# Attention block and PReLU layer on one core: the second product as seven products of halves, all steps placed anew

## The chip, the cores and the metric

One core of one Trainium2 chip. The metric is the device time of one execution in microseconds (us). Engines are TensorE (PE; its weight loads PEld), VectorE (DVE), ScalarE (ACT), GpSimd (POOL) and SyncE (SP, which only starts DMAs). TensorE writes its results to PSUM, here eight banks of 128 partitions by 512 f32 values; GpSimd works only on SBUF.

## The reference

```python
# x: 8 batches, 8 heads, 512 tokens, 64;  state: 8, 8, 32, 64
scores = scale * x @ state.T ;   a  = softmax(scores)  ; xread = a @ state
scores2 = scale * state @ x.T ;  a2 = softmax(scores2) ; sread = a2 @ x
X = concat([xread, sread], over tokens)      # 8 x (512 + 32) rows of 8*64 = 512
h = X @ w_in                                  # 512 -> 2048
g = max(h, 0) + alpha * min(h, 0)
out = g @ w_out                               # 2048 -> 512, f32
```

## The kernel before

The work goes batch by batch, and the 32 state rows of all eight batches (the "reads", 256 rows) make a ninth batch, number 8. Matmul operands are f16, PSUM is f32.

**One order written by hand.** ORDER (L17 to 99) is a list of steps; the loop at L666 runs it from the top, and each engine gets its instructions in that order and executes them in that order. A step is a name with arguments: `F.4.10.2` is the first product of batch 4, tile 10 of the 16 blocks of 128 of the 2048 columns, into bank k2. The steps that matter here:

- `lx` (L159) loads x of a batch from GpSimd's queue, casting to f16, into one of four xg buffers; `wi`, `wo` (L197, L203) load quarters of w_in and w_out the same way. `xd` (L276) transposes x by a DMA of SP's queue; `xt`/`xo` do it on TensorE for batches 0 and 1.
- `sc` (L296) makes the scores on TensorE. Over the states: `sb` (transpose, L334), `smax` (maximum, L367), `ssh` (shift, L372, on GpSimd for batches 1 to 7), `sexp` (L381), `ssum` (L385, L386), `snorm` (L389, GpSimd), `wb` (transpose back, L397). Over the tokens: `tm` (maximum L409, and a 128x2 scaling by -scale, L412, on VectorE), `te` (L420), `tsum` (L430), `tn` (scaling of e by 1/sum, L434, GpSimd), `tt` (DMA transpose, L438), `rd` and `rdo` (reads, L453, L464).
- `m`/`mo` (L480; L504 whole or L506 half) make state @ w_in per batch and quarter f of the 2048 columns, in f16: xread @ w_in is then a @ m.
- `F` (L517; for the reads L526): h of one tile, 128 x 512 (reads 128 x 256), into a bank. `N` (L572): ScalarE writes neg = relu(-h). `G` (L580): VectorE makes g = neg * (1 - alpha) + h, f16. `f`, `n`, `g` are the same in halves for the first tiles of batch 0.
- `S` (L595): second product. For a quarter q of a batch's rows, 128 rows by 512 output columns in one bank, summed over the 16 tiles of g: 16 matmuls of 512 columns, two per step. `O` (L611): a copy to SBUF by ScalarE or VectorE and an output DMA by SP. `R`/`RO` (L636, L646) are the same for the reads, `V`/`VO` (L618, L628) the last 128 columns of the last quarter.
- `Z` (L224): matmuls of zeros at the start.

PSUM: single banks k0 to k5, and a pair "two". A step that opens a bank waits until what read it last is done.

Of the kernel before, what the change touches and what calls it, by code (L numbers as in the profile page):

```python
# [17 lines left out]
stc wi.0 Z.0.9 stt.0 sbd.0.a lst sto.a cx.0.1.v sbd.1.a lx.1 cx.0.0.v Z.1.5 xt.0.0.1.0 oma  # L18
xt.0.0.0.1 xo.0.0.1.v wi.1 cx.1.0.a xo.0.0.0.v cx.1.1.v wo.0 Z.2.6 xt.0.1.0.0 tsc.0.0.1 xo.0.1.0.v
tsc.0.1 xt.0.1.1.2 wi.2 smax.0.0 sc.0.0 tsc.1.0.0 xo.0.1.1.a wo.1 ssh.v.0.0 Z.3.2 tsc.1.1 sc.0.1  # L20
wi.3 smax.0.1 sexp.0.0 Z.2.5 m.0.0.1.2 tm.0 wo.2 mo.0.0.a.1 mo.0.0.a.0 ssh.v.0.1 te.0.1 Z.3.11
str.1.1 lx.2 ssum.0.0 str.0.0 sexp.0.1 sro.1.a ssum.0.1 snorm.p.0.0 te.0.0 snorm.p.0.1 Z.2.13 at.0.1
sro.0.a xt.1.1.0.2 tsum.0 ao.0.v xt.1.1.1.3 tn.0.1 xt.1.0.0.4 xo.1.1.1.v at.1.1 xo.1.1.0.a f.0.0.0.5
xo.1.0.0.v m.1.0 ao.1.v n.0.0.0 m.2.0.4.2 xt.1.0.1.3 mo.1.0.v wo.3 mo.2.0.a.1 f.0.0.1.1 xo.1.0.1.a
f.0.1.1.0 tn.0.0 g.0.0.0.1 n.0.0.1 m.1.1 g.0.0.0.0 n.0.1.1 g.0.0.1.1 m.0.1.5.3 mo.1.1.a g.0.1.1.0
lx.3 tt.0 g.0.0.1.0 mo.0.1.a.1 g.0.1.1.1 sc.1 f.0.1.0.1 mo.0.1.a.0 sb.1 S.0.3.0.0 mo.2.0.a.0 F.0.4.3
n.0.1.0 F.0.5.2 tm.1 N.0.4 S.0.2.0.4 N.0.5 S.0.3.1 S.0.1.0.5 G.0.5 te.1.1 S.0.1.1 g.0.1.0.1 te.1.0
F.0.7.2 g.0.1.0.0 G.0.4 N.0.7 m.0.2 S.0.2.1 G.0.7 F.0.6.3 mo.0.2.v S.0.2.2 N.0.6 S.0.1.2 S.0.3.2
G.0.6 F.0.9.2 F.0.10.1 smax.1 N.0.9 F.0.8.3 N.0.10 S.0.3.3 N.0.8 G.0.9 m.0.3 ssh.p.1 S.0.2.3
mo.0.3.a G.0.10 F.0.11.2 G.0.8 S.0.1.3 N.0.11 F.0.14.1 tsum.1 sexp.1 F.0.12.3 tn.1.0 G.0.11 S.0.2.4  # L30
N.0.14 S.0.3.4 ssum.1 S.0.1.4 N.0.12 tn.1.1 S.0.1.5 S.0.2.5 G.0.14 F.0.13.2 m.1.2 snorm.p.1 G.0.12
xd.2 N.0.13 S.0.0.0.1 mo.1.2.a S.0.0.1 G.0.13 S.0.0.2 F.0.15.2 wb.1 S.0.0.3 N.0.15 S.0.0.4 S.0.1.6
G.0.15 F.1.4.3 S.0.0.5 N.1.4 S.0.1.7 F.1.0.2 G.1.4 O.0.1.a S.0.0.6 N.1.0 F.1.2.3 S.0.2.6 G.1.0 N.1.2
F.1.3.5 F.1.5.2 G.1.2 N.1.3 tt.1 S.0.0.7 N.1.5 F.1.1.3 G.1.3 S.0.2.7 xd.3 N.1.1 G.1.5 F.1.10.5 m.1.3
O.0.0.v N.1.10 rd.0.2 O.0.2.v mo.1.3.a F.1.6.1 lx.4 G.1.10 S.0.3.5 rdo.0.a N.1.6 sc.2 G.1.1
m.2.2.5.2 F.1.9.4 mo.2.2.a.0 tm.2 F.1.8.3 mo.2.2.a.1 S.0.3.6 N.1.9 S.1.0.0.2 G.1.6 N.1.8 S.0.3.7
te.2.0 G.1.9 S.1.0.1 F.1.11.1 te.2.1 G.1.8 F.1.7.4 N.1.11 S.1.0.2 tsum.2 sb.2 tn.2.1 N.1.7 F.1.13.3
rd.1.5 O.0.3.a G.1.7 N.1.13 xd.4 m.3.2 S.1.1.0.0 rdo.1.a lx.5 G.1.11 mo.3.2.a S.1.0.3 smax.2
F.1.12.5 tn.2.0 S.1.1.1 N.1.12 m.2.1 G.1.13 m.2.3.1.4 S.1.0.4 mo.2.1.a G.1.12 ssh.p.2 F.1.15.3 tt.2
mo.2.3.a.0 S.1.0.5 mo.2.3.v.1 N.1.15 F.1.14.5 S.1.1.2 G.1.15 N.1.14 S.1.1.3 sexp.2 S.1.1.4 G.1.14  # L40
S.1.0.6 sc.3 ssum.2 m.3.0.5.3 m.3.3.1.4 S.1.0.7 mo.3.0.a.0 xd.5 mo.3.0.a.1 S.1.1.5 tm.3 snorm.p.2
# [12 lines left out]
mo.5.0.v.0 mo.5.0.a.1 F.3.5.0 tn.4.0 G.3.2 sexp.4 m.5.2 m.4.2.1.5 S.2.2.3 mo.5.2.v N.3.5 S.2.2.4
tn.4.1 mo.4.2.a.1 F.3.4.2 mo.4.2.v.0 N.3.10 S.2.2.5 S.2.2.6 ssum.4 N.3.4 S.2.2.7 tt.4 S.2.3.0.1
S.2.3.1 G.3.10 snorm.p.4 S.2.3.2 G.3.5 S.2.3.3 F.3.13.4 G.3.4 S.2.3.4 N.3.13 O.2.2.v S.2.3.5
F.3.15.2 G.3.13 F.3.8.3 N.3.15 wb.4 m.6.0 N.3.8 m.5.3.4.0 rd.4.5 mo.6.0.a S.2.3.6 G.3.8 S.2.3.7
mo.5.3.a.1 rdo.4.v mo.5.3.v.0 F.4.0.3 O.2.3.a F.4.7.5 G.3.15 N.4.0 S.3.2.0.0 N.4.7 S.3.2.1 G.4.0
F.4.13.2 G.4.7 F.4.3.3 N.4.13 S.3.2.2 N.4.3 S.3.2.3 G.4.13 F.3.11.5 G.4.3 F.4.14.2 N.3.11 S.3.0.0.1
N.4.14 S.3.0.1 G.3.11 S.3.0.2 G.4.14 S.3.0.3 F.3.14.5 F.3.12.2 N.3.14 F.4.5.3 N.3.12 S.3.0.4 G.3.14  # L60
N.4.5 S.3.2.4 G.3.12 F.4.9.5 sc.5 G.4.5 N.4.9 m.7.0.2.4 S.3.2.5 xd.7 tm.5 mo.7.0.a.0 F.4.6.3 S.3.2.6
N.4.6 S.3.2.7 G.4.9 te.5.0 S.3.0.5 G.4.6 S.3.0.6 te.5.1 F.4.1.5 O.3.2.v F.4.4.3 N.4.1 sb.5 S.3.0.7
N.4.4 S.3.1.0.0 O.3.0.a S.3.1.1 G.4.1 S.3.1.2 smax.5 S.3.1.3 S.3.1.4 S.3.1.5 tsum.5 ssh.p.5 G.4.4
S.3.1.6 F.4.12.5 mo.7.0.v.1 F.4.8.3 N.4.12 S.3.1.7 N.4.8 F.4.2.2 G.4.12 tn.5.0 sexp.5 m.5.1 G.4.8
m.6.3.4.1 S.3.3.0.5 mo.6.3.a.0 mo.5.1.v S.3.3.1 tn.5.1 N.4.2 S.3.3.2 mo.6.3.a.1 S.3.3.3 G.4.2 sc.6
m.6.2.1.4 O.3.1.v tt.5 m.7.3.2.3 S.3.3.4 mo.7.3.a.0 mo.6.2.v.0 S.3.3.5 mo.7.3.a.1 mo.6.2.v.1
F.4.11.0 F.4.10.2 sb.6 N.4.11 S.4.3.0.1 N.4.10 S.3.3.6 S.3.3.7 G.4.10 F.4.15.4 O.3.3.a G.4.11
S.4.3.1 N.4.15 S.4.3.2 smax.6 S.4.1.0.0 S.4.3.3 G.4.15 S.4.3.4 ssh.p.6 S.4.1.1 ssum.5 S.4.1.2
S.4.1.3 m.7.2.4.5 sexp.6 m.6.1.2.3 tm.6 snorm.p.5 S.4.3.5 S.4.3.6 mo.7.2.a.1 S.4.3.7 mo.6.1.v.0
mo.6.1.a.1 S.4.1.4 te.6.1 O.4.3.v S.4.1.5 S.4.1.6 te.6.0 wb.5 S.4.1.7 S.4.0.0.1 S.4.0.1 O.4.1.v  # L70
F.5.0.2 ssum.6 F.5.5.0 N.5.0 S.4.0.2 N.5.5 F.5.7.3 mo.7.2.v.0 S.4.0.3 snorm.p.6 N.5.7 S.4.0.4 G.5.5
S.4.0.5 G.5.0 S.4.2.0.4 F.5.8.0 tsum.6 wb.6 tn.6.0 F.5.1.2 N.5.8 S.4.2.1 N.5.1 S.4.2.2 G.5.8 S.4.0.6
tn.6.1 S.4.2.3 G.5.1 F.5.14.0 G.5.7 F.6.3.2 N.5.14 S.4.2.4 tt.6 N.6.3 F.5.6.3 G.5.14 S.4.2.5 N.5.6
G.6.3 F.6.2.0 S.4.2.6 G.5.6 N.6.2 F.5.3.2 F.5.2.3 G.6.2 N.5.3 S.4.0.7 N.5.2 F.6.0.0 G.5.3 S.4.2.7
N.6.0 O.4.0.v F.5.13.2 O.4.2.a rd.6.5 G.6.0 N.5.13 rd.5.4 G.5.2 rdo.6.a F.5.12.0 rdo.5.a G.5.13
F.5.4.3 N.5.12 S.5.1.0.4 N.5.4 F.5.9.2 G.5.12 S.5.1.1 N.5.9 G.5.4 F.5.10.0 S.5.0.0.5 G.5.9 N.5.10
F.6.10.3 F.6.14.2 G.5.10 N.6.10 S.5.1.2 N.6.14 F.5.15.0 G.6.10 S.5.1.3 N.5.15 G.6.14 F.5.11.3
# [26 lines left out]
def kernel(  # L104
# [594 lines left out]
```

## Time and profile before

| | |
|---|---|
| device time, 3 runs | 223.12 us median (222.76 to 223.59) |
| span of the profiled execution, first to last instruction | 221.0 us |
| its own device time | not given; the median stands 2.1 us above the span |
| granted TensorE clock | 0.999 |
| busy: PE, DVE, ACT, POOL | 213.4, 171.1, 136.5, 69.7 us |
| L595 matmuls, 512 columns | 496, 123.1 us busy |
| L517 matmuls | 248, 66.9 us busy |
| L580 on VectorE, 128x512 | 124, 738 ns each |
| L572 on ScalarE, 128x512 | 124, 603 ns each |

The mean duration of a matmul row (379 ns for 512 columns) contains the pipeline; the distance between starts is what the next one waits for. The same holds, less strongly, for rows of the other engines. An engine's idle time counts only where a later engine waits for it.

### The profile page before, as it was taken

To read this page: it belongs to the slowest core of one execution; us is meant where nothing else is said; L and a number is where in the kernel's file an instruction comes from. 1 tells how busy PE (TensorE), PEld (TensorE's weight loads), DVE (VectorE), ACT (ScalarE), POOL (GpSimd) and SP (SyncE) were. 2 spreads that over 40 slices of the span, in tenths; PEclk is the share of its full clock that TensorE was granted. 3 is DMA by queue.
4 is the path that set the end of the run, shared out by engine and by line. 5 is a ranking of instruction groups with operands and counts; after the bars stand their busy time and mean duration, and the time that the engine had idled before them with its cause. 6 is when DMAs were issued, how large, how long until landed. Compare 5 with 4: busy or idle time off the path is not lost.

```text
span 221.0 us, 4301 instructions
## 1 busy us (share of the span) xinstructions
PE 213.4 (97%) x1683; PEld 103.1 (47%) x1683; DVE 171.1 (77%) x258; ACT 136.5 (62%) x259; POOL 69.7 (32%) x55
## 2 busy tenths in 40 slices
PE   5997999999999999999999999999999999999994
PEld 3774434444444444344443434454445455544443
DVE  1689998699899989998798999998988538753011
ACT  2399874799866968947557465587763446571110
POOL 3978056028466500830017155300353000000000
PEclk9999999999999999999999999999999999999999
DMA  6999999989999195131080502220131111010222
GB/s 178 156 194 206 200 190 194 193 168 205 193 228 140 51 141 142 49 98 49 18 175 0 142 18 81 47 98 0 49 95 52 47 47 50 0 61 34 108 85 95
DMA packets 49220, 23.65 MB, mean 107 GB/s; under 512 B 38448, under 2 KB 44976, under 8 KB 49200
## 3 DMA queue, kind: packets, MB, share of 16 engines
q0 software_dynamic: 18816, 8.09, 29.5%
q1 hardware_dynamic: 30112, 15.22, 27.2%
q8 instruction: 13, 0.21, 0.4%
q10 hardware_dynamic: 272, 0.07, 0.1%
q14 instruction: 7, 0.06, 0.1%
HBM read 17.31 MB, written 8.91 MB: 119 GB/s over the span
## 4 chain that ended last, share of the span: by engine, by line
PE 87%; DVE 5%; DMA 3%; ACT 3%; issue 1%; POOL 0%; SPq 0%; ACTq 0%
PE o L595 44%; PE h L517 24%; PE m_ps L480 3%; PE h L526 3%; PE o L636 3%; PE z L224 3%; PE sr_ps L453 2%; DMA st<-in_state_dram 2%; DMA e2T<-e 2%; PE sc L303 1%; PE xT_ps L288 1%; DVE nb L409 1%; DVE gt L580 1%; ACT neg L554 1%; ACT e L420 1%
## 5 line engine op out<-in xcount | busy, mean ns | idle before, releaser
L595 PE MATMUL o<-w_out_sb,gt 128*128 128x512 f16 (+1 forms) x512 | 125.7, 378 | 0.0
L572 ACT ACTIVATE neg<-h 128x512 f32<-128x512 f32 (+1 forms) x140 | 75.6, 578 | 43.6 <-PE h L517 36.5
L580 DVE SCALAR_TENSOR_TENSOR gt<-neg,oma_sb,h 128x512 f16<-128x512 f32 x124 | 87.3, 738 | 18.2 <-ACT neg L572 16.7
L595 PEld LDWEIGHTS <-gt 128*128 128x128 f16 x512 | 48.5, 98 | 58.7 <-issue 5.5
L517 PE MATMUL h<-aT,m 128*128 128x512 f16 x248 | 66.9, 379 | 0.1
L517 PEld LDWEIGHTS <-m 128*128 128x128 f16 x248 | 23.8, 98 | 28.8 <-issue 0.8
L434 POOL TENSOR_SCALAR e<-e,r 128x512 f16<-128x512 f16 x16 | 24.9, 1561 | 22.7 <-DVE r L430 22.3
L372 POOL TENSOR_TENSOR ts<-ts,mx 128x1024 f32<-128x1024 f32 x7 | 13.4, 1909 | 45.0 <-DVE mx L367 26.1
L611 ACT COPY osb<-o 128x512 f32<-128x512 f32 x20 | 11.8, 592 | 16.3 <-PE o L595 16.3
L389 POOL TENSOR_TENSOR an<-ts,r 128x1024 f16<-128x1024 f32 (+1 forms) x9 | 15.4, 1719 | 16.8 <-DVE r L386 16.8
L611 DVE COPY osb<-o 128x512 f32<-128x512 f32 (+1 forms) x12 | 7.9, 664 | 12.9 <-PE o L595 12.9
L506 ACT CAST m<-m_ps 128x512 f16<-128x512 f32 x27 | 15.1, 600 | 2.4 <-PE m_ps L480 2.4
L161 POOL DMA_DIRECT2D xg<-in_x_dram x7 | 8.4, 1199 | 11.1 <-PE sr_ps L453 10.8
L420 ACT ACTIVATE e<-sc,nb 128x512 f16<-128x512 f32 x16 | 10.9, 693 | 1.4 <-DVE nb L412 1.3
L480 PE MATMUL m_ps<-w_in_sb,stT 64*32 64x512 f16 x256 | 11.2, 381 | 0.5 <-DVE gt L560 0.4
L381 ACT ACTIVATE ts<-ts 128x1024 f32<-128x1024 f32 (+1 forms) x9 | 8.7, 964 | 3.6 <-POOL ts L372 2.9
L385 DVE TENSOR_REDUCE r<-ts 128x32 f32<-128x1024 f32 (+1 forms) x9 | 9.9, 1096 | 0.4 <-ACT ts L381 0.2
L224 PE MATMUL z<-zero 128*128 128x256 f16 x51 | 8.9, 330 | 1.3 <-DVE zero L218 1.3
L409 DVE TENSOR_REDUCE nb<-sc 128x2 f32<-128x1024 f32 x8 | 9.6, 1199 | 0.5 <-PE sc L303 0.5
L580 DVE SCALAR_TENSOR_TENSOR gs<-neg,oma_sb,h 128x256 f16<-128x256 f32 x16 | 7.5, 476 | 3.3 <-ACT neg L572 3.3
L504 ACT CAST m<-m_ps 128x1024 f16<-128x1024 f32 x9 | 9.2, 1028 | 0.8 <-PE m_ps L480 0.7
L526 PE MATMUL h<-XS,w_in_sb 128*128 128x256 f16 x64 | 9.1, 273 | 0.0
(61 smaller groups left out, 140.4 us busy)
## 6 DMA issues: line engine op xcount, KB each, us to landing
out_dram<-osb SPq DMA_DIRECT2D x31, 256.0 KB, 2.1
xg<-in_x_dram POOLq DMA_DIRECT2D x7, 512.0 KB, 8.1
w_in_sb<-in_moe_w_in_dram POOLq DMA_DIRECT2D x4, 512.0 KB, 12.2
w_out_sb<-in_moe_w_out_dram POOLq DMA_DIRECT2D x4, 512.0 KB, 18.2
x<-in_x_dram SPq DMA_DIRECT2D x2, 512.0 KB, 4.6
out_dram<-osr SPq DMA_DIRECT2D x2, 256.0 KB, 2.5
st<-in_state_dram POOLq DMA_DIRECT2D x1, 224.0 KB, 6.6
out_dram<-osb SPq DMA_DIRECT2D x1, 192.0 KB, 2.0
```

What stands on the lines that cost most here:

```text
L224: nc.tensor.matmul(t, zero[:, :128], zero, start=True, stop=True)
L372: engine(e).tensor_tensor(blocks(cols(live["ts", b], j, S)), blocks(scored(b, j)), over_blocks(cols(live["mx", b], j, S // N)), ALU.subtract,)
L389: engine(e).tensor_tensor(blocks(cols(live["an", b], j, S)), blocks(cols(live["ts", b], j, S)), over_blocks(cols(live["r1", b], j, S // N) ...
L434: nc.gpsimd.tensor_scalar_mul(e2, e2, live["r2", b][:, g : g + 1])
L480: nc.tensor.matmul(t[N * k : N * (k + 1), :], st_head(b, h)[64 * r : 64 * r + 64, :], w_in_sb[64 * r : 64 * r + 64, c, 512 * f : 512 * (f ...
L506: copier(e)(m_tile(b, f)[:, g, :], t[g])
L517: nc.tensor.matmul(h.rearrange("p (r j s) -> p r j s", r=2, j=2), ms[b, f][:, g, 128 * j : 128 * (j + 1)], weights(b, g), start=(g == 0), ...
L526: nc.tensor.matmul(h, w_in_sb[:, c, 128 * jc : 128 * (jc + 1)], XS[:, c].rearrange("p q n b -> p (q n b)"), start=(c == 0), stop=(c == n_c ...
L572: nc.scalar.activation(neg, h, RELU, bias=0.0, scale=-1.0)
L580: nc.vector.scalar_tensor_tensor(gt, negs.pop((b, jc)), oma_sb[:, jc : jc + 1], h, ALU.mult, ALU.add)
L595: nc.tensor.matmul(outs[b, q], gts[b, jc][:, 128 * q : 128 * (q + 1)], w_out_sb[:, jc, :w], start=(jc == 0), stop=(jc == n_jc - 1),)
L611: copier(e)(osb, t)
```

## The change

With g of a batch split into halves of rows and of the 2048 columns, and w_out into halves of its 2048 rows and of its 512 columns, the second product is a product of 2 x 2 blocks. Batches 1 to 7 and the reads now take it by seven block products and sums (Strassen, in Winograd's form of four sums on each side) instead of eight block products. Batch 0 keeps `S` and `O`.

- `W` makes four sums of blocks of w_out, once: three on GpSimd, one on VectorE, 128x2048 f16.
- `U` makes four sums of g per batch, each in two parts c (128x1024 f16; reads 128x512). 48 of the 64 are on GpSimd, 16 on VectorE.
- `P` does four matmuls of 256 columns: product p, row block i of 128, part c. A batch has 28 such steps (112 matmuls), the reads 14.
- Three banks per batch: products 1, 6, 5 and 3 are summed in bank x, 4 and 7 in v, 2 in y. Between them `K` copies the state of x to SBUF three times per batch. `Q` adds a bank and a kept copy on VectorE and writes the quarter out; one quarter per batch is a plain copy of x.
- Sizes: xg buffers 4 to 3; m tiles per quarter 8, 5, 5, 5 to 4, 3, 3, 3; the g tiles of four become one tile each.
- `tn` becomes a two-operation instruction, with a second multiplication by 1.0.
- ORDER is a new list. Among its differences: the first `wi` stands ahead of the state cast `stc` on GpSimd's queue; the later `wi` and `wo` come after the first `snorm`; the first `W` of GpSimd comes after `snorm.p.1`, and `lx.3` after two of the three; all `mo` but one are on ScalarE.

```diff
-        xg = xgs[b] = att.tile([128, H, 2, 2, D], F16, name=f"xg_{b}", tag="xg", bufs=4)
+        xg = xgs[b] = att.tile([128, H, 2, 2, D], F16, name=f"xg_{b}", tag="xg", bufs=3)
...
-        nc.gpsimd.tensor_scalar_mul(e2, e2, live["r2", b][:, g : g + 1])
+        nc.gpsimd.tensor_scalar(
+            e2, e2, live["r2", b][:, g : g + 1], 1.0, ALU.mult, ALU.mult
+        )
...
-                [128, 2, 512], F16, name=f"m_{b}_{f}", tag=f"m{f}", bufs=(8, 5, 5, 5)[f]
+                [128, 2, 512], F16, name=f"m_{b}_{f}", tag=f"m{f}", bufs=(4, 3, 3, 3)[f]
...
+    W_SUMS = {
+        1: ((0, 1), (0, 0)),
+        3: ((1, 1), (0, 1)),
+        2: ((1, 1), 1),
+        4: ((1, 0), 2),
+    }
+    def w_sum(i, e):
+        a, c = W_SUMS[i]
+        t = ws[i] = consts.tile([128, n_h, d_h], F16, name=f"ws_{i}")
+        engine(e).tensor_tensor(t, w_halves[a], ws[c] if c in ws else w_halves[c], ALU.subtract)
...
+    def g_sum(b, i, c, e):
+        w = S // 2 if b < B else B * N // 2
+        t = gss[b, i, c] = moe.tile(
+            [128, 4, w], F16, name=f"gsum_{b}_{i}_{c}", tag=f"gsum{i}{c}", bufs=1
+        )
+        x, y, op = {
+            1: (lambda: g_half(b, 1, c), lambda: g_half(b, 1, 2 + c), ALU.add),
+            2: (lambda: gss[b, 1, c], lambda: g_half(b, 0, c), ALU.subtract),
+            3: (lambda: g_half(b, 0, c), lambda: g_half(b, 1, c), ALU.subtract),
+            4: (lambda: g_half(b, 0, 2 + c), lambda: gss[b, 2, c], ALU.subtract),
+        }[i]
+        engine(e).tensor_tensor(t, x(), y(), op)
+    PRODUCTS = {
+        1: ("x", lambda b, c: g_half(b, 0, c), (0, 0)),
+        2: ("y", lambda b, c: g_half(b, 0, 2 + c), (1, 0)),
+        3: ("x", lambda b, c: gss[b, 4, c], (1, 1)),
+        4: ("v", lambda b, c: g_half(b, 1, 2 + c), 4),
+        5: ("x", lambda b, c: gss[b, 1, c], 1),
+        6: ("x", lambda b, c: gss[b, 2, c], 2),
+        7: ("v", lambda b, c: gss[b, 3, c], 3),
+    }
+    def product(b, p, i, c, k=None):
+        name, of, w = PRODUCTS[p]
+        n_i = 2 if b < B else 1
+        begun = (b, name) in pbanks
+        if not begun:
+            pbanks[b, name] = single(k, f"p{name}_{b}", [128, n_i, d_h], F32)
+        moving = ws[w] if w in ws else w_halves[w]
+        for j in range(4):
+            nc.tensor.matmul(
+                pbanks[b, name][:, i, :],
+                of(b, c)[:, j, 128 * i : 128 * (i + 1)],
+                moving[:, 4 * c + j, :],
+                start=not begun and j == 0,
+                stop=True,
+                skip_group_check=True,
+            )
+    def keep(b, name, e):
+        n_i = 2 if b < B else 1
+        t = kept[b, name] = moe.tile(
+            [128, n_i, d_h], F32, name=f"kept_{name}_{b}", tag=f"kept{name}", bufs=1
+        )
+        copier(e)(t, pbanks[b, "x"])
...
+    def quarter_out(b, th, dh, e=None):
+        n_i = 2 if b < B else 1
+        name, add = {(0, 0): ("y", 1), (0, 1): ("x", None), (1, 0): ("v", 2), (1, 1): ("v", 4)}[th, dh]
+        osb = moe.tile([128, n_i, d_h], F32, name=f"oq_{b}_{th}_{dh}", tag="osb", bufs=4)
+        if add is None:
+            copier(e)(osb, pbanks[b, name])
+        else:
+            nc.vector.tensor_tensor(osb, pbanks[b, name], kept[b, add], ALU.add)
+        nc.sync.dma_start(quarter_rows(b, th, dh), osb if b < B else osb[:, 0, :])
```

A stretch of the new ORDER, in which products of batch 4, first products of batches 5 and 6 and softmax steps alternate:

```
P.4.6.0.0 te.6.1 P.4.6.1.1 P.4.6.0.1 K.4.2.a te.6.0 tsum.6 tn.6.1 F.5.13.1 N.5.13 G.5.13 P.4.2.0.0 P.4.5.1.0 F.5.12.5
N.5.12 F.5.8.0 N.5.8 P.4.5.1.1 tt.5 sc.7 P.4.7.1.1.4 G.5.12 G.5.8 snorm.p.6 P.4.7.0.1 P.4.2.1.0 Q.4.0.0 F.5.4.1 N.5.4
```

## The prediction

> **What bounds the kernel now.** I read the page's busy times first, then the chain that ended last, then the busy times of the middle stretch, then the groups with shapes kept apart.
>
> ```profile
> PE 213.4 (97%) x1683; PEld 103.1 (47%) x1683; DVE 171.1 (77%) x258; ACT 136.5 (62%) x259; POOL 69.7 (32%) x55
> ...
> PE 87%; DVE 5%; DMA 3%; ACT 3%; issue 1%; POOL 0%; SPq 0%; ACTq 0%
> ```
>
> ```profile
> 30.00:170.00 140.00, 139.38 (x1134) 62.12 (x1127) 128.22 (x182) 97.83 (x183) 52.97 (x32) 1.00 0.60 108
> ```
>
> From 30 to 170 us TensorE (first busy figure, then weight loads, VectorE, ScalarE, GpSimd) is idle for 0.6 of 140 us at full granted clock (1.00). So TensorE's work is the time: 213.4 busy and 7.6 idle, nearly all of that before 21 us and in the last 3.1. VectorE, with 128.2 of 140, is the next limit.
>
> A busy TensorE is not yet a price. That comes from the distance between starts of back-to-back matmuls, in the timeline and in the chain of waits:
>
> ```profile
> 99.76 1.03 PE L517 MATMUL h<-aT,m 128*128 128x512 f16 x4
> 100.62 1.03 PE L595 MATMUL o<-w_out_sb,gt 128*128 128x512 f16 x4
> 101.48 1.03 PE L517 MATMUL h<-aT,m 128*128 128x512 f16 x4
> ```
>
> ```profile
> 177.21 0.87 PE h L526 x8
> ...
> 188.04 0.87 PE h L526 x8
> ```
>
> Four matmuls of 512 columns start every 0.863 us: 0.216 each. Eight of 256 columns, each with weights of its own, take 0.87: 0.109 each. Half the columns cost half the time, and a weight load (row PEld L526, 98 ns) still fits beneath.
>
> **The change, part by part**
>
> **The products.** Before: 496 + 32 matmuls of 512 columns at 0.216 (114.0 us), 16 of 384 at 0.163 (row 326 ns less the 163 by which a row outlasts its spacing; 2.6), 16 of 128 (0.91): 117.5 us. After: batch 0 keeps 64 at 0.216 (13.8), and seven batches of 112 plus 56 for the reads make 840 of 256 columns at 0.109 (91.6): 105.4. TensorE loses **12.1 us**: 1.6 in each of seven batches, 0.8 in the reads. Everything else on it has the same counts. The span would be 221.0 - 12.1 = 208.9. The profiled execution's own time is not given; the median of 223.12 is 2.1 above its span, so 211.0 is the floor.
>
> **GpSimd.** Its rows:
>
> ```profile
> L434 POOL TENSOR_SCALAR e<-e,r 128x512 f16<-128x512 f16 x16 | 24.9, 1561 | 22.7 <-DVE r L430 22.3 <-ACT neg L572 0.2
> L389 POOL TENSOR_TENSOR an<-ts,r 128x1024 f16<-128x1024 f32 x7 | 13.4, 1911 | 16.1 <-DVE r L386 16.1
> L372 POOL TENSOR_TENSOR ts<-ts,mx 128x1024 f32<-128x1024 f32 x7 | 13.4, 1909 | 45.0 <-DVE mx L367 26.1 <-DVE r L430 18.9
> ...
> L389 POOL TENSOR_TENSOR an<-ts,r 128x512 f16<-128x512 f32 x2 | 2.1, 1047 | 0.7 <-DVE r L386 0.7
> ```
>
> It receives 45 sums of g of 1024 columns, 3 of 512, and three sums of w_out of 2048. The two-input rows give 1.91 for 1024 and 1.05 for 512, so 3.64 for 2048: 86.0 + 3.1 + 10.9 = 100 us on top of 69.7. The f16 operands of a g sum are not in the trace. Below: the affine select on 128 f16 columns (0.291) sits with the f32 cast of that size (0.289), so f16 is at least no dearer to read: 1.9. Above: the 3.05 ns per column of row L434, 3.1. I take 1.91, the same operation and size. The scaling of e gets a second multiplication by 1.0: between 0.6 (the select's 0.291 stretched to 512 by 0.8 ns a column) and the old 1.56; I take the two-input 1.05.
>
> Is this hidden? GpSimd can't start early: the scores' shift (L372) waits for the maxima until 29.8 and ends at 31.7, as before. Counted from there to the last sum of batch 4 that TensorE needs (U.4.4.0): 27 sums, 3 of w_out, 5 shifts and 6 norms at 1.91, 12 scalings at 1.05, 6 x issues at 1.2 = 103.3, so 135.0 us. TensorE's own work ahead of the product that takes it (P.4.3.1.0) is 127.5; its actual starts run 8.0 behind this sum throughout (sc of batch 5 at 108.48 against 100.5), so 135.5. The same sum reaches U.1.2.0 at 59.8, against 58.7 on TensorE. Cover is nil: GpSimd runs level with TensorE, about 1 late. Loading x of batch 3 now stands behind two of the w_out sums (three x buffers instead of four): issue at 47.1, landing 7.4 (the tile's median), transposing DMA 5.1 (its median) = 59.6, while TensorE reaches those scores at 58.2: 1.4 late, and every matmul queues behind that wait. Bounds for both together: 0 (scalings at 0.6, landing at its minimum of 3.6) to 6 (scalings at 1.56). These waits share one delay: I take 1.3.
>
> **VectorE.** It gives up 11 copies of o (0.67), one of 0.56 and one of reads (0.69), 3 whole and 11 half m casts (1.22, 0.68), and three transposed-tile copies (0.4): 21. It gets 24 output additions from PSUM (21 like L580's 0.74, 3 like its 0.48: 17.0), 16 sums of g, one of w_out, stT's copies (2.5) and four small copies (2.2). A g sum of 1024 in f16 lies between 0.65 (f16 copies of 512 take 0.418, against 0.673 in f32) and 1.2 (reductions of 1024 in f32); I take 0.65, the f16 row. Summed at back-to-back spacings (0.66 for L580) up to the last first-product of batch 5, VectorE has 132 us of work against TensorE's 134; before, 133 against 143. The margin of 10 has become 2.
>
> One wait eats it. When GpSimd is busy, a tiny VectorE operation does this:
>
> ```profile
> 59.79 1.91 POOL L389 TENSOR_TENSOR an<-ts,r 128x1024 f16<-128x1024 f32 x1 [2.93 <-DVE r L386]
> ...
> 60.76 0.97 DVE L412 TENSOR_SCALAR nb<-nb 128x2 f32<-128x2 f32 x1
> ```
>
> The 128x2 scaling, else 0.169, ends at 61.73, just after GpSimd's instruction (61.70). Two of eight did so (mean 368 ns, median 169) with GpSimd 38% busy; with GpSimd level with TensorE nearly all eight would, some 0.8 each, 4 of them by batch 5: 3 us. VectorE is then about 1 late, its L580 queueing behind. Bounds: 0 to 5. I take 1.
>
> The Trainium skill, "SBUF — State Buffer", section "Who interferes with whom", says the same of this row, and speaks against more of the change: a VectorE instruction with two SBUF inputs also waits out a GpSimd instruction that reads SBUF, and blocks it in turn. That would add up to 0.95 to each of the 17 sums on VectorE, an estimate from that page's rule and the 1.91 row; seven stand before the end of batch 5, so some 5 us more there, and the sum by it would be near 219. No row here shows it.
>
> **ScalarE** loses 18 output copies and two wide stT copies and gains 21 kept partial sums (0.59), 7 quarter copies and 14 m casts; 137 becomes about 152, hidden. But 24 keeps stand between products in one bank. Eight leave TensorE 0.87 us of other work; a keep needs 0.16 + 0.59 + about 0.05 = 0.81 (matmul tail, row L611, release of sc after L504). Bounds 0 to 4; I take 0.6.
>
> **Start and end.** The first w_in load moves ahead of the state cast, 4.6 to about 1.3 us, into the two x loads that the first chain needs: -0.5 to 2; I take 0.6. The later weights are issued after the first norm; at the rate seen (the fourth w_in landed at 29.4 with 5.2 MB queued ahead) they land no later than before. The end keeps one small copy and DMA: 0. SP has 36 output DMAs instead of 35, and the x transposes it moves past keep their data waits.
>
> Sum: 208.9 + 0.6 + 1.3 + 1 + 0.6 = 212.4; with 2.1, **214.5 us**.
>
> **Rivals**
>
> *Nothing waits* (0.13): all covers hold, 211.0, with a quicker start 210. For: TensorE idles 0.6 in 140 now. Against: three engines level with it.
>
> *VectorE becomes the bound* (0.10): sums at 1.2 instead of 0.65 (seven by batch 5, one of them double: 4.4) on the forecast: 219. The rule above gives the same.
>
> *GpSimd's sums are slower, and the change loses* (0.17). Ahead of P.4.3.1.0 stand 27 sums and three w_out sums worth 5.7: 33 units with no cover. Each 0.1 us costs 3.3; the gain of 8.6 is gone at 1.91 + 0.26 = 2.17 per sum. At 2.25 the time is 225, at 3.1 over 250. For: both two-input rows have a repeated second operand; these sums read two whole tensors. Against: f16 halves the bytes.
>
> The skill's "GPSIMD Engine Reference", section 3.1, gives 4497 ns for a 2048-column addition: half of it, 2.25, is an estimate from that page, and would make 225. The 1.91 rows disagree with it so far.
>
> *The change doesn't deliver* (0.03): 256-column matmuls at L526's busy time by count, 9.1/64 = 0.142, add 840 x 0.033 = 28: 239. Runs of eight in 0.87 speak against it.
>
> **The numbers.** The forecast, 212 to 218, has 0.55; some 0.02 is left over. A measurement of this kernel tells 0.5% (1.1 us) from no change. Faster than 222.0: 0.55 + 0.13 + 0.10, so 0.78. GpSimd's rival splits into 0.05 within 0.5% and 0.12 above; with the last one and the rest 0.06 and 0.16. The range from 210.5 to 221 holds the first three cases and a little of the fourth.
>
> **What would show it.** Four products every 0.44 us: the saving holds; 0.57 and it doesn't. GpSimd's g sums at 1.9 or 2.2 and more decide the sign. nb scalings near 1 us show the port wait. Idle TensorE before sc of batch 3 shows the x chain, before P after K the keeps, before F or P on "DVE" VectorE as the bound. A TensorE busy under 97% with none of these would prove me wrong.

## The result and the profile after

The change makes the kernel slower: 245.78 us median (244.24 to 247.37, 4 runs) against 223.36 for the kernel before, measured beside it, ratio 1.101 (95% interval 1.095 to 1.107). The forecast was 214.5, range 210.5 to 221. The profiled execution took 244.24 us, its span is 242.3, the mean granted clock 0.978 (0.999 before).

The page of the changed kernel: busy times, then the shares of the chain of work that ended last.

```profile
PE 211.5 (87%) x2027; PEld 138.6 (57%) x2027; DVE 195.6 (81%) x276; ACT 148.2 (61%) x283; POOL 169.3 (70%) x106
...
PE 58%; DVE 20%; DMA 8%; POOL 7%; issue 4%; ACT 2%; SPq 1%; ACTq 0%; DVEq 0%; POOLq 0%
```

Its busy times from 30 to 170 us:

```profile
30.00:170.00 140.00, 121.98 (x1163) 72.16 (x1164) 124.07 (x158) 99.98 (x187) 114.28 (x64) 0.96 0.62 107
```

Before, TensorE was busy for 139.38 of these 140 us and held 87% of the chain; now for 121.98 and 58%. VectorE took 20% of the chain, 5% before, yet it is busy for less of this stretch (124.07 against 128.22): it is late rather than full. The clock column says 0.96 where it said 1.00. So the new matmuls are not the loss. Their spacing, in the timeline:

```profile
161.04 0.60 PE L678 MATMUL pv<-ws,gsum 128*128 128x256 f16 x4
161.48 1.04 PE L678 MATMUL px<-ws,gsum 128*128 128x256 f16 x8
162.35 0.60 PE L678 MATMUL pv<-ws,gsum 128*128 128x256 f16 x4
162.79 0.38 PE L527 MATMUL h<-aT,m 128*128 128x512 f16 x1
```

Four products start every 0.44 us, 0.109 each: the saving of 12.1 us of TensorE's work is real. What eats it stands in the list of TensorE's waits (engine, tile and line, who released it, total, times, longest):

```profile
PE h L527 <- DVE g L583: 6.9, 3, 4.1
PE sr_ps L451 <- DMA e2T<-e: 5.5, 1, 5.5
PE px L678 <- ACT kept L694: 2.2, 2, 2.0
PE tsc L337 <- DVE xT L289: 2.1, 1, 2.1
...
PE pv L678 <- DVE gsum L657: 1.4, 1, 1.4
...
PE px L678 <- POOL gsum L657: 0.7, 1, 0.7
```

Of these only the last two, 2.1 us together, are products that wait for a sum of g. The largest is a first product `F` whose bank VectorE has not read yet. The timeline around it:

```profile
53.48 1.21 POOL L157 DMA_DIRECT2D xg<-in_x_dram  x1
...
53.76 5.06 DVE L408 TENSOR_SCALAR nb<-nb 128x2 f32<-128x2 f32 x1
54.72 4.06 POOL L638 TENSOR_TENSOR ws<-w_out_sb,ws 128x2048 f16<-128x2048 f16 x1
...
59.90 1.36 DVE L583 SCALAR_TENSOR_TENSOR g<-neg,oma_sb,h 128x512 f16<-128x512 f32 x2
60.65 0.79 PE L527 MATMUL h<-aT,m 128*128 128x512 f16 x2 [4.15 <-DVE g L583]
```

The scaling of two columns (nb, the row maximum times -scale, which the exponential takes), 0.17 us by itself, starts while GpSimd issues the load of x, is held through that and the whole sum of w_out behind it, and ends at 58.82, just after the sum (58.78). VectorE's queue stands still for 5 us, and TensorE for 4.15. The groups of the new operations, first on GpSimd, then on VectorE:

```profile
L657 POOL TENSOR_TENSOR gsum<-g,g 128x1024 f16<-128x1024 f16 x9 | 19.1, 2125 | 10.9 <-DVE g L583 9.1 <-PE h L536 1.8
...
L430 POOL TENSOR_SCALAR e<-e,r 128x512 f16<-128x512 f16 x16 | 11.4, 719 | 3.2 <-ACT oq L709 1.6 <-ACT neg L580 1.6
L638 POOL TENSOR_TENSOR ws<-w_out_sb,ws 128x2048 f16<-128x2048 f16 x2 | 9.0, 4500 | 0.1
```

```profile
L408 DVE TENSOR_SCALAR nb<-nb 128x2 f32<-128x2 f32 x8 | 9.7, 1208 | 0.3
...
L657 DVE TENSOR_TENSOR gsum<-g,gsum 128x1024 f16<-128x1024 f16 x3 | 5.0, 1668 | 0.0
L638 DVE TENSOR_TENSOR ws<-w_out_sb 128x2048 f16<-128x2048 f16 x1 | 3.3, 3286 | 0.0
```

A sum of g takes 2.13 on GpSimd; on VectorE its row has a mean of 1.67 for three, where the one at 72.96 us in the timeline, with GpSimd idle until 73.19, takes 0.63. The second large wait is a transfer: the DMA that transposes the token weights e into e2T. In the timeline:

```profile
83.52 1.63 SPq L276 DMA_TRANSPOSE xT<-xg  x1
83.92 0.16 DVE L426 RECIPROCAL r<-r 128x2 f32<-128x2 f32 x1
84.24 1.35 POOL L430 TENSOR_SCALAR e<-e,r 128x512 f16<-128x512 f16 x2 [1.61 <-ACT oq L709]
...
85.55 1.21 POOL L157 DMA_DIRECT2D xg<-in_x_dram  x1
86.43 1.75 SPq L436 DMA_TRANSPOSE e2T<-e  x1
...
94.21 1.00 PE L451 MATMUL sr_ps<-e2T,xg 128*64 128x32 f16 x31 [5.46 <-DMA e2T<-e]
```

ScalarE has finished e of batch 3 at 76.9. Its reciprocal stands seven us deeper in VectorE's order, the scalings follow, and the transposing DMA starts beside a transpose and a load of x and needs 7.6 us (from the chain; the median of its kind is 3.1). The state reads of batch 3 wait 5.46 us for it. The start is late too, in the timeline:

```profile
12.52 0.17 DVE L255 TENSOR_SCALAR oma_sb<-alpha_sb 128x16 f32<-128x16 f32 x1 [4.59 <-DMA alpha_sb<-in_moe_alpha_dram]
12.60 0.42 DVE L289 COPY xT<-xT_ps 128x512 f16<-128x512 f16 x1
...
13.08 0.61 PE L337 MATMUL tsc<-st_pairs,xT 128*128 128x64 f16 x8 [2.13 <-DVE xT L289]
```

And the two longest waits are paid twice. Busy time of TensorE and granted clock behind the wait that ends at 60.65, by stretch:

```profile
57.00:61.00 4.00, 0.35 (x2) 0.99 1.01 151
61.00:62.00 1.00, 1.00 (x6) 0.50 1.27 289
62.00:63.00 1.00, 1.00 (x5) 0.50 0.98 219
63.00:64.00 1.00, 1.00 (x4) 0.50 0.00 0
64.00:65.00 1.00, 1.00 (x6) 0.84 0.07 16
```

TensorE runs at half clock for 3.4 us: 1.7 more lost, with all its work at hand. Behind the wait of 5.46 it does so for 4.3 us. The other waits of this execution, one of 2.13 and one of 1.97 among them, leave the clock at 1.00.

### The profile page after: what moved, and what is told of

It reads as the page before. It is cut to its first block, busy times and chain, and to the rows that moved or that the text cites. A ratio compares the mean times of both kernels' runs of the same rounds, so it can differ in the third digit from the quotient of the medians.

```text
span 242.3 us, 5080 instructions
## 1 busy us (share of the span) xinstructions
PE 211.5 (87%) x2027; PEld 138.6 (57%) x2027; DVE 195.6 (81%) x276; ACT 148.2 (61%) x283; POOL 169.3 (70%) x106
## 4 chain that ended last, share of the span: by engine, by line
PE 58%; DVE 20%; DMA 8%; POOL 7%; issue 4%; ACT 2%; SPq 1%; ACTq 0%; DVEq 0%; POOLq 0%
PE px L678 19%; PE h L527 15%; PE pv L678 8%; DMA alpha_sb<-in_moe_alpha_dram 4%; POOL gsum L657 4%; DVE g L583 4%; PE py L678 4%; DVE nb L408 3%; DVE gsum L657 3%; DMA e2T<-e 3%; PE m_ps L478 3%; PE h L536 2%; DVE nb L405 2%; DVE ts L330 2%; PE o L597 1%
## 5 line engine op out<-in xcount | busy, mean ns | idle before, releaser
L583 DVE SCALAR_TENSOR_TENSOR g<-neg,oma_sb,h 128x512 f16<-128x512 f32 (+1 forms) x140 | 93.3, 708 | 14.0 <-ACT neg L580 12.9
L678 PEld LDWEIGHTS <-gsum 128*128 128x128 f16 x480 | 45.9, 98 | 18.4 <-issue 4.4
L678 PEld LDWEIGHTS <-g 128*128 128x128 f16 x360 | 34.7, 99 | 12.5 <-issue 3.1
L657 POOL TENSOR_TENSOR gsum<-g 128x1024 f16<-128x1024 f16 x13 | 28.1, 2158 | 9.6 <-DVE g L583 8.0
L678 PE MATMUL px<-ws,gsum 128*128 128x256 f16 x240 | 31.6, 273 | 3.0 <-ACT kept L694 2.2
L657 POOL TENSOR_TENSOR gsum<-g,gsum 128x1024 f16<-128x1024 f16 (+1 forms) x13 | 26.0, 2005 | 5.5 <-PE px L678 5.3
L657 POOL TENSOR_TENSOR gsum<-gsum,g 128x1024 f16<-128x1024 f16 x12 | 26.0, 2164 | 3.4 <-DVE gsum L657 2.9
L657 POOL TENSOR_TENSOR gsum<-g,g 128x1024 f16<-128x1024 f16 (+1 forms) x10 | 20.3, 2028 | 10.9 <-DVE g L583 9.1
L694 ACT COPY kept<-px 128x512 f32<-128x512 f32 (+1 forms) x21 | 12.2, 580 | 14.5 <-PE px L678 9.8
L678 PE MATMUL px<-w_out_sb,g 128*128 128x256 f16 x120 | 18.5, 287 | 0.0
L678 PE MATMUL pv<-ws,gsum 128*128 128x256 f16 x120 | 16.9, 273 | 1.4 <-DVE gsum L657 1.4
L597 PE MATMUL o<-w_out_sb,g 128*128 128x512 f16 x64 | 17.8, 392 | 0.0
L416 ACT ACTIVATE e<-sc,nb 128x512 f16<-128x512 f32 x16 | 11.0, 694 | 10.2 <-DVE ts L330 4.8
```

What stands on the lines that cost most here:

```text
L416: nc.scalar.activation(live["e2", b][:, g, :, :], live["sc", b][:, :, :, g, :].rearrange("p r j s -> p (r j) s"), EXP, bias=live["nb", b][ ...
L583: nc.vector.scalar_tensor_tensor(g_tile(b, jc), negs.pop((b, jc)), oma_sb[:, jc : jc + 1], hs.pop((b, jc)), ALU.mult, ALU.add,)
L597: nc.tensor.matmul(outs[b, q], g_tile(b, jc)[:, 128 * q : 128 * (q + 1)], w_out_sb[:, jc, :], start=not begun and jc == 2 * jc2, stop=left ...
L657: engine(e).tensor_tensor(t, x(), y(), op)
L678: nc.tensor.matmul(pbanks[b, name][:, i, :], of(b, c)[:, j, 128 * i : 128 * (i + 1)], moving[:, 4 * c + j, :], start=not begun and j == 0, ...
L694: copier(e)(t, pbanks[b, "x"])
```

## The experiments

All runs, each measured beside the kernel before (222.6 to 226.6 us over all its runs):

| kernel | median us | ratio to before (95%) |
|---|---|---|
| changed kernel | 245.78 | 1.095 to 1.107 |
| e1_no_sums | 228.85 | 1.021 to 1.034 |
| e2_sums_unread | 245.72 | 1.093 to 1.108 |
| e3_start | 243.43 | 1.089 to 1.093 |
| e4_nb_act | 245.36 | 1.094 to 1.103 |
| e5_vector_sums_only | 230.34 | 1.023 to 1.034 |
| e6_gpsimd_sums_only | 237.12 | 1.053 to 1.067 |
| e7_place_no_sums | 220.81 | 0.981 to 0.991 |
| e8_place | 236.38 | 1.047 to 1.061 |
| e9_place_nb | 233.33 | 1.036 to 1.048 |
| e10_w_vector | 236.33 | 1.050 to 1.061 |
| e11_place_no_sums2 | 218.68 | 0.974 to 0.981 |
| e12_reads_plain | 236.49 | 1.052 to 1.065 |
| e13_nb_later | 231.63 | 1.034 to 1.041 |
| e14_no_w_sums | 229.87 | 1.025 to 1.033 |
| e15_no_g_sums | 225.35 | 1.006 to 1.011 |
| e16_tail_vector | 230.50 | 1.028 to 1.037 |
| e17_all_vector | 260.90 | 1.155 to 1.174 |
| e18_late_vector | 238.02 | 1.062 to 1.069 |

My theory after reading the trace: the sums cost by what they do to VectorE and to GpSimd's other work, through the port that both use. Rivals: products wait for late sums; or the sums cost little, and the new placing of the other steps is the loss.

**e1: no sums.** All `W` and `U` steps leave ORDER, and

```diff
-        3: ("x", lambda b, c: gss[b, 4, c], (1, 1)),
+        3: ("x", lambda b, c: g_half(b, 0, 2 + c), (1, 1)),
...
-        5: ("x", lambda b, c: gss[b, 1, c], 1),
+        5: ("x", lambda b, c: g_half(b, 1, c), (0, 1)),
```

(4, 6 and 7 likewise).

> The changed kernel without any of the sums of g and of w_out (all U and W steps go; the products read halves of g and of w_out in their place, so the output is not the reference's). Its TensorE work, its order and its other steps stay. If the sums cause the loss, by whatever way (they hold the port that VectorE needs, or they come late, or they keep GpSimd from other work), what stays of the 33 us over the floor of 208.9 is the start (5.0 us of lag, 0.6 of it in the forecast), the late e2T of batch 3 (5.5) and ScalarE's waits (about 4): 211 + 5 + 5.5 + 4, so 217 to 226. If the loss comes from the new placing and the moved transfers, it keeps at least 235.

228.85. Both are at work: the sums cost 16.9 us, and 17.9 over the floor of 211.0 remain without any. This run shows the clock most plainly, since its wait is short (busy time of TensorE, clock):

```profile
121.00:123.00 2.00, 0.06 (x1) 1.00 0.00 0
123.00:124.00 1.00, 1.00 (x10) 1.00 0.00 0
124.00:125.00 1.00, 1.00 (x7) 0.55 0.00 0
125.00:127.00 2.00, 2.00 (x14) 0.50 0.00 0
127.00:128.00 1.00, 1.00 (x6) 0.74 0.08 16
```

A wait of 1.99, from 120.95 to 122.94, and half clock for 3.4 us, beginning 1.2 us after work is back.

**e2: sums made, not read.** The edit of the products as in e1; `W` and `U` stay.

> The sums are computed as in the changed kernel, on the same engines in the same places, but the products read halves of g and of w_out in their place (the output is not the reference's). If TensorE loses its time by waiting for late sums, this gives nearly what the kernel without sums gives (within 3 us of it). If the loss is what the sums do to VectorE and to GpSimd's other work (VectorE's two-input sums at up to 2.5 us where 0.6 was taken, its scaling of nb at 5.06, tn and descriptors behind sums on GpSimd), it stays within 5 us of 245.

245.72, the changed kernel's time. TensorE's waits there:

```profile
PE h L527 <- DVE g L583: 6.9, 3, 4.1
PE sr_ps L451 <- DMA e2T<-e: 6.3, 1, 6.3
PE px L678 <- ACT kept L694: 4.1, 2, 2.2
```

Nobody waits for a sum, and the 6.9 behind VectorE's g stand as before. The 2.1 us that products waited for sums don't come back: a wait for a keep (a copy `K` of a bank) stands at the end in their place, 4.1 in all instead of 2.2. The rival of late sums falls, as far as a spread of some 3 us in the runs of either kernel lets one see: the sums' results are in time, or nearly; their making is the cost.

**e5 and e6: one engine's sums alone.** Products as in e1; of the sums only those with `.v`, or only those with `.p`, stay. A sum whose input was left out reads the half of g in its place.

> The changed kernel with VectorE's seventeen sums alone (one of w_out, sixteen of g); GpSimd's forty-eight sums of g and three of w_out are left out, and the products read halves of g and of w_out (the output is not the reference's). It stands between the kernel without sums (228.9) and the one with all of them unread (245.7). If the cost of the sums lies in GpSimd's instructions, by their length, by what waits behind them on GpSimd and by the port that they hold, VectorE's own sums run at their undisturbed 0.63 (1024) and about 1.3 (2048), 10 us spread over the program: 228 to 232. If VectorE's load as such is the cost, 238 or more.

> The other half: GpSimd's sums alone, VectorE's seventeen left out, products as before on halves of g and w_out (the output is not the reference's). If only the meeting of two-input sums of both engines costs, this falls to 228 to 233. If GpSimd's sums cost by themselves (the scaling of nb still waits behind them, and GpSimd's tn, its shift and its descriptors come later), it stays at 238 to 246.

230.34 and 237.12: over the kernel without sums, VectorE's seventeen cost 1.5 us (less than the 3.4 by which that kernel's own runs differ), GpSimd's fifty-one 8.3 (between the two ranges of the expectation), both together 16.9. The 7.1 that neither makes alone arise when both are there. VectorE's groups, without sums on GpSimd:

```profile
L404 DVE TENSOR_SCALAR nb<-nb 128x2 f32<-128x2 f32 x8 | 2.0, 253 | 0.3
...
L634 DVE TENSOR_TENSOR ws<-w_out_sb 128x2048 f16<-128x2048 f16 x1 | 1.2, 1212 | 0.0
```

and with sums on GpSimd alone:

```profile
L407 DVE TENSOR_SCALAR nb<-nb 128x2 f32<-128x2 f32 x8 | 12.3, 1534 | 0.3
```

The sum of w_out falls from 3.29 to 1.21, the scaling from 1208 ns to 253; with GpSimd's sums back it is 1534: there one scaling is held for 6.05 us, through four GpSimd instructions, and TensorE waits 4.97 us behind it. How the 8.3 divide between such scalings and GpSimd's other, later steps no run shows. The meeting of two sums, in the timeline of the changed kernel:

```profile
219.68 2.60 POOL L657 TENSOR_TENSOR gsum<-gsum,g 128x1024 f16<-128x1024 f16 x1
220.34 2.49 DVE L657 TENSOR_TENSOR gsum<-gsum,g 128x1024 f16<-128x1024 f16 x1
...
222.36 2.45 POOL L657 TENSOR_TENSOR gsum<-g,gsum 128x1024 f16<-128x1024 f16 x1
```

VectorE's sum, 0.66 in e5, starts under GpSimd's and ends 0.55 after it, at 222.83; GpSimd's next takes 2.45 where 2.13 is usual. VectorE's seventeen sums take 10.9 us in e5 and 20.4 here. The Trainium skill, "SBUF — State Buffer", section "Who interferes with whom", has this rule: the two engines share a port pair, held for a whole instruction, and VectorE needs it for an instruction with two SBUF inputs, where GpSimd reads SBUF too, and for a scaling in its two-port mode. By that rule, the traces agree, with these rows; the forecast had given it a place and then too little weight.

**e3 and e4: one suspect each.**

```diff
-wi.0 stc Z.0.9 ... cx.0.1.v oma xt.0.0.1.1 ... ssh.v.0.1 Z.1.5
+stc wi.0 Z.0.9 ... cx.0.1.v xt.0.0.1.1 ... ssh.v.0.1 oma Z.1.5
```

```diff
-        nc.vector.tensor_scalar_mul(nb, nb, -scale)
+        nc.scalar.mul(nb, nb, -scale)
```

> Two steps go back to where they were: the cast of the first states stands ahead of the first read of w_in, and 1 - alpha, whose DMA lands at 12.5 us, stands behind the state shift of batch 0, so that nothing of VectorE's start waits for alpha. If the new order of the start costs what the lag of TensorE at its first scores of batch 1 shows (12.2 against 7.2), the time falls by 4 to 5 us, to 240 to 242. If a later bound (GpSimd's sums, VectorE behind them) takes the lag up, it falls by less than 2.

> The scaling of nb (128 x 2), 9.7 us over its eight on VectorE with one at 5.06, goes to ScalarE; nothing else changes. If GpSimd's use of the port holds VectorE there, TensorE's wait of 4.15 at 60.65 goes, and the others shrink: 3 to 6 us less, 239 to 242. If VectorE would have waited anyway (its next two-input sum meets the same GpSimd instruction), less than 2 us are won.

243.43 and 245.36: 2.3 us, and 0.4, which is inside the spread. By total both theories lose; the starts show why. In the trace of e3 the scores of batch 1 start at 23.9 in place of 26.3, and those of batch 3 at 69.1 in place of 71.8. In that of e4 it takes 15.6 us from the scores of batch 2 to those of batch 3, 19.8 in the changed kernel: the 4 us of nb are won there. But from the scores of batch 1 to those of batch 2 it takes 28.6 us, 25.8 in the changed kernel: with nb on ScalarE, TensorE waits 0.45 and 0.64 more near 30 us, and 3.4 us at half clock follow. So e4 is 1.9 ahead at the scores of batch 3. The state reads of batch 3 start at 94.2 in the changed kernel, at 93.3 in e3 and at 94.0 in e4: the late e2T, for which they wait 7.0 and 6.5 in place of 5.5, takes most of what is left. A cure must be tried with that wait gone.

**e7 and e8: four places put back,** without and with the sums.

```diff
-smax.3 ssh.p.3 P.1.5.1.0 ... G.2.3 tsum.3 tn.3.1 tn.3.0 sexp.3 ... lx.6 ... tt.3
+smax.3 tsum.3 tn.3.1 tn.3.0 tt.3 xd.4 ssh.p.3 P.1.5.1.0 ... G.2.3 sexp.3 ... lx.6 ...
...
-sb.5 P.3.1.1.0 F.4.3.5 te.5.1 ... te.5.0
+P.3.1.1.0 F.4.3.5 te.5.1 ... te.5.0 sb.5
```

(`sb.1` and `sb.4` likewise, and the start of e3.)

> The kernel without sums (228.9), with four places put back: the first states' cast ahead of the first read of w_in; 1 - alpha behind the state shift of batch 0; the reciprocal, the two scalings and the transposing DMA of batch 3's token weights behind the row maximum of batch 3, ahead of the sixth x load; the score transposes of batches 1, 4 and 5 on VectorE behind ScalarE's exponentials of the same scores, for which ScalarE waited 2.48 at 121.64 in the kernel without sums. Again the output is not the reference's. If the placing holds what is left over the floor of 211 there (about 18 us: start 5, e2T of batch 3 with the half clock behind it 7, the wait at 122.94 with its half clock 3.7), this gives 214 to 219. If each of these waits hides another bound behind it, it stays above 223.

> The changed kernel with all its sums and the same four places put back. If placing and sums add up, it gains what the kernel without sums gains, 10 to 14 us: 231 to 235, still slower than before. If the sums set the pace by themselves (VectorE and GpSimd fall behind whatever TensorE does), it gains less than 5: over 240.

220.81 and 236.38: 8.0 and 9.4 us won. Placing and sums add up; neither hides the other. Both stand 1.4 to 1.8 above the ranges expected, and the head of e7's list of waits has a reason that I made: moving `sb.1` gave a wait of 2.1, with half clock from 28.9 to 32.3 behind it, in place of one of 1.4 with full clock.

```profile
PE m_ps L472 <- DVE r L420: 2.1, 1, 2.1
```

**e11: three places, no sums;** **e9, e13: three places, sums, nb on ScalarE.** `sb.1` is where the change has it; e9 has the edit of e4, e13 keeps nb on VectorE for batches 0 and 1:

```diff
+        if b > 1:
+            nc.scalar.mul(nb, nb, -scale)
+        else:
             nc.vector.tensor_scalar_mul(nb, nb, -scale)
```

> The three places put back without the transpose of batch 1, and no sums (the products read halves of g and w_out; the output is not the reference's). If the wait of 2.07 at 29.12 and the half clock behind it were made by that one move, 3 to 4 us less than 220.8: 216.5 to 218. If the wait is due to the start, 220 or more.

> The changed kernel with its sums, with the start, batch 3's token steps and the score transposes of batches 4 and 5 put back (the transpose of batch 1, which cost a wait of 2.07 at 29.12 and 3.9 us at half clock in the kernel with four places put back, stays where the change has it), and with the scaling of nb on ScalarE. If nb on VectorE is held by GpSimd's port, the wait of 4.15 at 60.30 of that kernel and its 3.3 us at half clock go: 5.8 us, and with some 3 for the transpose 236.4 - 8.8, so 226 to 230. If VectorE's next two-input sum takes up what nb leaves, 232 or more.

> The kernel with three places put back and nb's scaling on ScalarE (233.3), but with the scaling of batches 0 and 1, where GpSimd has no sums yet, on VectorE again. If nb on ScalarE made the waits of 0.45 and 0.64 at 26 and 27.9 and the half clock behind them, 2 to 3 us less: 230 to 231.5. If not, 232.5 or more.

218.68, 233.33 and 231.63. e11, somewhat above what was expected, is what the products could be worth in this order if sums were free: 4.8 us less than before, about 2%, with TensorE's share back up on its page:

```profile
PE 205.6 (95%) x2027; PEld 137.7 (64%) x2027; DVE 168.9 (78%) x259; ACT 147.8 (68%) x283; POOL 56.0 (26%) x55
```

e9 missed its range of 226 to 230 and stands where the other case of its expectation put it, 232 or more; e13 stands just above its own: nb on ScalarE in the first two batches costs 1.7 us by the medians. Part of that is the clock: two of e9's four runs granted 0.990 and took 234.2 and 234.4, the two at 0.998 and 1.000 took 232.4, 0.8 above e13.

**e14 and e15: which sums?** e13 without the sums of w_out, and without those of g.

> The same kernel without the four sums of w_out; the products that need them read halves of w_out (the output is not the reference's); all sums of g stay. TensorE's lag grows from 38 to 68 us by 8 us in the kernel with sums and by 2 without, and W.1, W.2 and W.4 hold GpSimd for 13 us of that stretch, W.3 VectorE for 3.3. If the sums of w_out are most of the cost, 6 to 8 us less than the kernel with all sums. If it is the sums of g, under 3 less.

> The same kernel without the sixty-four sums of g (the products read halves of g; the output is not the reference's); the four sums of w_out stay. The lag from 70 us to the end grows by 7.3 + 9.7 with sums and by 4 + 3.5 without. If the sums of g cost in each batch, 7 to 9 us less than the kernel with all sums, near 222 to 224. If the sums of w_out are the cost, it stays above 226.

229.87 and 225.35: leaving out the sums of w_out wins 1.8 us, leaving out those of g 6.3 (a little less than expected), leaving out both (e11 against e13) 13.0. So each kind hides a part of the other's cost: beside e11, the sums of w_out alone stand 6.7 higher, those of g alone 11.2, both 13.0 and not 17.9. e11 keeps nb on VectorE in all batches, so a part of each figure is that move. With nb off VectorE the long wait at 60 us is gone, and the sixty-four sums of g, spread over the batches, are the larger part.

**e10, e12, e16, e17, e18: another engine for some sums, or none for the reads.** e10 and e12 start from e9 (`W.1`, `W.2`, `W.4` to `.v`; e12 in addition does the reads as `S` with 512 columns), the others from e13 (`U` to `.v` for batches 7 and 8, for all with `W` too, for 5 to 8).

> As the kernel with the scaling of nb on ScalarE, and all four sums of w_out on VectorE, none on GpSimd: GpSimd loses 13 us there, VectorE gains three times 1.3 (an estimate: twice its undisturbed 0.63 for half as many elements). If the meeting of two-input sums of both engines is what costs there (3.29 in place of 1.3 and a wait of 1.53 of TensorE), this gains 1 to 4 us over it. If VectorE's load is the limit between 44 and 62 us, it loses 1 to 4.

> As the kernel with all sums of w_out on VectorE, and the reads' second product in the form of before: 32 matmuls of 512 columns in the places of the seven products, none of their eight sums. TensorE gains 0.8 us of work; the sums at the end of the program go, 3 us of which TensorE's lag at the end shows over that of the kernel without sums. If those sums set the end, 1 to 3 us less than the kernel before it in this list; if not, 0.8 more.

> The same kernel with the sums of batch 7 and of the reads all on VectorE (sixteen, of which GpSimd had seven). VectorE's two at 2.50 and 2.49, which meet sums on GpSimd, fall to 0.65, and those moved to it cost 0.65 or 0.42 each in place of 2.12 or 1.16 on GpSimd. If the meeting sets the end (3.3 us more lag at the end than without sums), 2 to 4 us less. If the end waits for the last products and outputs anyhow, under 1 less.

> The kernel with three places put back and nb of batches 2 to 7 on ScalarE (231.6), with all sixty-eight sums on VectorE and none on GpSimd, in the same places of the order. VectorE's busy time without sums is 169; fifty-six sums at 0.63, eight at 0.42 and four at some 1.3 (an estimate, twice 0.63) make 213. If GpSimd's share is what costs, by length and by meeting, the time falls towards that: 221 to 228. If VectorE's queue is the limit (it is 90% busy from 40 to 190 us already), 233 or more.

> The same kernel with the sums of batches 5 to 7 and of the reads all on VectorE, those of batches 1 to 4 and of w_out where the change has them. If meeting and GpSimd's length are the cost, batches 5 and 6 win some 1 us each on top of the 1.1 that batch 7 and the reads gave: 228 to 229.5. If VectorE becomes late there, 231 or more.

e10 loses 3.0, e12 nothing more (0.2: either the reads' sums and TensorE's 0.8 cancel, or neither counts), e16 wins 1.1 (2 to 4 were expected), e18 loses 6.4, and e17, with every sum on VectorE, those of g under 1 us each by the means of its rows and those of w_out 1.22, loses 29 us. Its busy times from 40 to 70 (TensorE, weight loads, VectorE, ScalarE, GpSimd):

```profile
40.00:70.00 30.00, 25.38 (x262) 13.08 (x260) 28.22 (x36) 20.38 (x40) 6.35 (x6) 1.00 0.70 117
```

VectorE has no room there: 28.2 of 30. Sums in the same places of its order push g back and come late themselves: over the whole of e17 TensorE waits 6.6 us for sums of g and 5.3 for g. So GpSimd's length and port are one price and VectorE's queue is another, and only at the end, where VectorE is less busy (e16: 20.7 of 30 from 190 to 220), is moving a sum a gain. None of the kernels with all its sums beats the one before.

## Why the prediction was wrong, step by step

The runs make a ladder. Floor of the forecast: 211.0. Order with three places put back, no sums: 218.7. As the change places it, no sums: 228.9. With sums: 245.8, of which VectorE's alone 1.5, GpSimd's alone 8.3, both at once 7.1 more. The forecast had 3.5 for all of these 34.8. So its direction was wrong, and two steps of it failed: what GpSimd's and VectorE's sums do to each other and to small steps (16.9), and the new places of old steps (10.2 for the three put back).

- **The products: right.** 0.109 each, which for 840 makes the 12.1 us reckoned.
- **GpSimd, the first failed step: "Cover is nil: GpSimd runs level with TensorE, about 1 late."** Its prices were fair: 2.13 against the 1.91 taken, 4.06 to 4.94 against 3.64 for w_out, 0.72 against 1.05 for the scaling of e. What failed is comparing two sums of work, as if GpSimd met TensorE only where a product takes a sum. By e2 that meeting costs nothing that shows. The cost sits in what shares GpSimd's port and queue: nb and VectorE's own sums, as their rows show, and, by an amount that no run divides off, GpSimd's later steps. The x load of batch 3, priced 1.4 late, made no wait that the list shows, as TensorE itself was 14 late by then (scores of batch 3 at 71.8 in place of the 58.2 reckoned).
- **VectorE: "VectorE is then about 1 late ... I take 1", with bounds 0 to 5.** The mechanism was named and seen in a row; the size was wrong. I priced a held scaling at 0.8, one GpSimd instruction; the eight took 9.7 in all, 8.3 more than eight at 0.169, and one was held through two GpSimd instructions in a row, 5.06. With VectorE's margin at 2 by the forecast's own count, a value near the lower bound was not the place to stand.
- **The Trainium skill's rule on two SBUF inputs: right where no row showed it.** 0.63 to 0.71 for 1024 columns by the means of e5's rows, up to 2.52 in a meeting; 7.1 us by e1, e5 and e6 against the changed kernel, where 5 were worked out from it for the first five batches.
- **"GpSimd's sums are slower, and the change loses": the sign was right, the point was not.** At 2.13 the break-even of 2.17 was not reached; that rival's own arithmetic gives 33 x 0.22 = 7.3 more, about 222. The Trainium skill, "GPSIMD Engine Reference", section 3.1, had 4497 ns for 2048 columns, 2.25 by half, an estimate; here 1024 took 2.13, nearer to that than to my row, and 2048 took 4.06 undisturbed, midway between its figure and my 3.64.
- **The start: 0.6 taken, bounds -0.5 to 2.** The scores of batch 1 start 12.2 us behind TensorE's own work ahead of them (reckoned with the prediction's prices), 7.2 in the kernel before: 5.0 lost. I priced the read of w_in moved ahead by the x loads that it joins, not by alpha: `oma` (1 - alpha) stands ahead of a transposed tile's copy in VectorE's order, as it did before, and its DMA now lands 10.6 us after its issue (5.6 before). In e3, with the read of w_in back behind the cast, it lands after 5.7: the moved read held alpha back. e3 wins 2.4 of the lag at the scores.
- **Steps that the sum did not have, with the start the second failed step.** The reciprocal, scalings and transposing DMA of batch 3's token weights were moved; I counted their costs, not the time between their inputs and their place. 5.46 us of wait, with 4.3 us at half clock behind it. Nor was there a term for the clock, which had stood at 0.999.
- **The keeps on ScalarE: 0.6, bounds 0 to 4.** 2.2 of wait, most of it 1.97 at one place, where ScalarE waits for VectorE's transpose of the same scores ahead of it.

What stays open: of the 7.7 us between the floor and e11, the waits listed in its trace explain less than half. TensorE is busy for 205.6 us there, 7.8 less than before and not 12.1, and idle for 3.6 more; where the busy time beyond the reckoned one lies, no view here shows. Nor was batch 3's DMA put back alone.

## What to carry to other kernels

When work moves to an idle engine, ask first which ports and queues that engine shares, and price every small instruction that needs them at one of that engine's long instructions, and at a run of neighbouring ones for the upper bound. A margin between two engines' totals is no cover: what counts is the distance, at each place of the order, between the time when an input is ready and the step that uses it, and the engine with 2 us to spare takes nothing more. To find a loss that hides behind another, take the sums out and put the order back separately, and look at starts inside the program where the total doesn't move.

## What the runs showed of the hardware

- **Half clock after a short wait, but not after each.** A wait of 1.99 us (e1) was followed by 3.4 us at 0.50. The same wait in e5, ending at 123.05, left the clock at 1.00, and so did one of 1.97 in the changed kernel, ending at 133.77. After the 5.46 it lasted from 91.6 to 98.5, 6.8 us, twice as long. The Trainium skill, "TensorE: Matmul & The Clock Gate", Part 1, gives the same half rate and a window of 3.4 us that runs freely; it asks for an idle window, and here a wait shorter than one sufficed. A wait of 1.36 left it at full in e11, and 3.4 us at half clock followed it in the profiled executions of e4 and e9, where waits of 0.45 and 0.64 stood in the four us ahead of it; yet two of e9's four runs had a mean of 0.998 and 1.000. What decides it, no run here shows. In the changed kernel the mean of 0.978 over 242.3 us makes 5.3 us, of which 1.3 fell into the wait of 5.46 itself.
- **A held VectorE instruction may have to wait for several GpSimd instructions, but need not:** the scaling of two columns was held through an x load's issue and a sum, 5.06 us, and through four instructions in e6, 6.05. In the changed kernel three such scalings (at 74.75, 102.92 and 154.20) ended 0.03 us after one GpSimd instruction, though the next followed at once. The sum of w_out on VectorE, once it had the port, in turn stretched GpSimd's from 4.06 to 4.94.
- **A second operation made GpSimd's scaling cheaper:** 719 ns for `tensor_scalar` with two operations, 1561 with one, same shape and type (each of the sixteen with one took 1552 to 1574).
